# Linear attention on one core: later stores, part of relu(k) on GpSimd, eps added by 32-row matmuls, and a rewritten order of work

## The chip, the cores and the metric

The kernel runs on one core of one Trainium2 chip. The metric is the device time of one execution in microseconds. The kernel before took 180.35 us in the median of three runs (179.49, 180.35 and 180.47). The profiled execution, from which every duration in this text comes, took 179.64 us, and its span from the first to the last instruction is 177.9 us.

## The reference

Everything is bf16, with B=1, H=32 heads, S=2048 rows and D=128 columns.

```python
phi_q = jnp.where(q > 0, q + 1, jnp.exp(q)) + 1e-6
phi_k = jnp.where(k > 0, k + 1, jnp.exp(k)) + 1e-6
kv  = jnp.einsum("bhsd,bhse->bhde", phi_k, v)
z   = jnp.einsum("bhsd->bhd", phi_k)
num = jnp.einsum("bhqd,bhde->bhqe", phi_q, kv)
den = jnp.einsum("bhqd,bhd->bhq", phi_q, z)[..., None] + 1e-6
return num / den
```

Each of q, k, v and the output holds 16.8 MB, 512 KB per head, so that a head moves 2 MB and the whole kernel 67.1 MB.

## The kernel before

A head is split into 16 tiles of 128 rows. The feature map is written as phi(x) = min(exp(x), 1) + eps + relu(x), and the two summands are never added: TensorE multiplies by both of them and adds the products up in PSUM. One head h goes through these steps; each has a name that is used from here on.

- `ldk`, `ldq`, `ldv` (line 238): loads on SP's queue into rings of NI=8 heads. The load of head h+8 waits until head h has been read (`ek`, `rk`, `T`, `v1`).
- `ek` (line 347): ScalarE, exp(k) into `em_sb`. `em` (line 331): VectorE, min and eps in place, two heads in one instruction from head 4 on. `rk` (line 339): VectorE, relu(k) into `rk_sb`, also in pairs.
- `v1` (line 378): GpSimd copies v beside a column of ones, as 32-bit words. From head 3 on it waits for the reciprocal `rA` of three heads earlier.
- `kx`, `kv` (line 362): 32 matmuls build kv and z (129 columns) in one PSUM region. `kvs` (line 373): ScalarE copies it to SBUF.
- `T` (line 354): 16 transposes of q into the one PSUM buffer `xT`. `eq` (line 394): ScalarE, exp. `rqa` (line 399): ScalarE, relu of the first half of the columns; `rqb` (line 402): VectorE, relu of the second half. In every fourth head (an "A" in `RELU_Q = "SSSA"`) ScalarE does both halves in one wide `rqa` and there is no `rqb`. `emq` (line 406): VectorE, min and eps.
- `nB`, `nA`, `nC`: the numerators with the denominator as column 129. In each of six PSUM banks a small matmul of a matrix of ones by `epsr` (line 277, 128 rows, 2 or 3 columns) sets the denominators to eps, and then 2 matmuls per tile (lines 281 and 283) add the products, 32 in a head.
- `rA`, `rC` (line 303): reciprocals. `fA`, `fC` (line 307): VectorE multiplies the numerators in PSUM by them, 12 and 4 tiles, into `o_sb`, a ring of NO=6 heads. `st` (line 251) stores a head from there, and `fA` and `fC` wait for the store of six heads earlier.

The last two heads are cut into three parts each (D, B, C), and ScalarE scales the C part (line 324).

No loop runs on the chip. The order of each engine's queue is a list written out by hand in `SCHEDULE` (`PE`, `DVE`, `ACT`, `POOL`); a further list `kv` is the order in which the engines use the PSUM banks that kv and the last four tiles share. `Program.resolve` turns dependences across engines into semaphore waits. SP's queue is in the order of the program: after the first 8 heads, each turn gives three loads of head h+8 and, with `LAG = 2`, the store of head h-2:

```python
for h in range(NH + LAG - 1):
    if h + NI < NH:
        loads(h + NI)
    if h >= LAG:
        store(h - LAG)
```

Matmuls on a unit matrix (`warm0` with 48, `warm1` with 22; line 437) run before the first transposes and between them and the second ones.

Of the kernel before, what the change touches and what calls it, by code (L numbers as in the profile page):

```python
# [15 lines left out]
class Program:  # L16
# [20 lines left out]
    def resolve(self):  # L37
# [5 lines left out]
        for bank, keys in self.banks.items():  # L43
            order = self.schedule[bank]
            assert sorted(order) == sorted(keys), (bank, set(order) ^ set(keys))
            for a, b in zip(order, order[1:]):
                if self.ops[a]["eng"] != self.ops[b]["eng"]:
                    self.ops[b]["deps"].append(a)
        value, count = {}, {}
# [48 lines left out]
def _eps_pieces():  # L98

    import struct  # L100

    def bf(x):
        u = struct.unpack("<I", struct.pack("<f", x))[0]
        u = (u + 0x7FFF + ((u >> 16) & 1)) & 0xFFFF0000
        return struct.unpack("<f", struct.pack("<I", u))[0]

    a = bf(EPS / 128)
    b = bf(EPS - 126 * a)
    return a, b, bf(EPS - 126 * a - b)


def bass_standalone__linear_attn_elu__prompt_kernel(nc: bass.Bass, q: bass.AP, k: bass.AP, v: bass.AP, out: bass.AP):
# [8 lines left out]
    NO = 6  # L121
    L = NH - 1

    LAG = 2
    VLAG = 3
    VAFTER = "rA"
    VFROM = 3
    VTO = 31
    LATE = {L - 1: dict(D="DVE", B="DVE", C="ACT"), L: dict(D="DVE", B="DVE", C="ACT")}
    V1_DVE = 1  # L130
    FUSED = [0] * NH
# [4 lines left out]
    WARM1 = 22  # L136
    FIRST = [("k", 0), ("q", 0), ("v", 0)]
    RELU_Q = "SSSA" * (NH // 4)
# [3 lines left out]
            "warm0 T0 warm1 T1 kx0 kv0 nC0 nA0 T2 nB0 kx1 kv1 nC1 kx2 kv2 nA1 T3 nC2 nB1 kx3 kv3 nB2 nA2 T4 nC3 kx4 kv4 nB3 "  # L142
            "nA3 T5 nC4 kx5 kv5 nB4 nA4 T6 nC5 kx6 kv6 nB5 nA5 T7 nC6 kx7 kv7 nB6 nA6 T8 nC7 kx8 kv8 nB7 nA7 T9 nC8 kx9 kv9 "
            "nB8 nA8 T10 nC9 kx10 kv10 nB9 nA9 T11 nC10 kx11 kv11 nB10 nA10 T12 nC11 kx12 kv12 nB11 nA11 T13 nC12 kx13 kv13 "
            "nB12 nA12 T14 nC13 kx14 kv14 nB13 nA13 T15 nC14 kx15 kv15 nB14 nA14 T16 nC15 kx16 kv16 nB15 nA15 T17 nC16 kx17 "
            "kv17 nB16 nA16 T18 nC17 kx18 kv18 nB17 nA17 T19 nC18 kx19 kv19 nB18 nA18 T20 nC19 kx20 kv20 nB19 nA19 T21 nC20 "
            "kx21 kv21 nB20 nA20 T22 nC21 kx22 kv22 nB21 nA21 T23 nC22 kx23 kv23 nB22 nA22 T24 nC23 kx24 kv24 nB23 nA23 T25 "
            "nC24 kx25 kv25 nB24 nA24 T26 nC25 kx26 kv26 nB25 nA25 T27 nC26 kx27 kv27 nB26 nA26 T28 nC27 kx28 kv28 nB27 nA27 "
            "T29 kx29 kv29 nB28 nA28 T30 nC28 kx30 kv30 nA29 nB29 nC29 T31 kx31 kv31 nD30 nC30 nB30 nD31 nC31 nB31 ").split(),
        DVE=(  # L150
            "eps0 ones v1ones0 v1ones1 eps1 eps2 rk0 em0 emq0 rqb0 rk1 v10 emq1 rqb1 rk2 rC0 fC0 em1 em2 rk3 rqb2 emq2 rA0 "
            "fA0 em3 rC1 fC1 rk5 rC2 fC2 em5 rA1 fA1 emq3 rA2 fA2 rk7 rC3 fC3 rqb4 emq4 rA3 fA3 em7 rC4 emq5 rqb5 fC4 rA4 fA4 "
            "rk9 rC5 rqb6 emq6 fC5 rA5 fA5 em9 rC6 fC6 emq7 rA6 fA6 rk11 rC7 rqb8 emq8 fC7 rA7 fA7 em11 rC8 rqb9 emq9 fC8 rA8 "
            "fA8 rk13 rC9 rqb10 emq10 fC9 rA9 fA9 em13 rC10 emq11 fC10 rA10 fA10 rk15 rC11 rqb12 emq12 fC11 rA11 fA11 em15 "
            "rC12 rqb13 emq13 fC12 rA12 fA12 rqb14 rC13 emq14 fC13 rk17 rA13 fA13 emq15 rC14 fC14 em17 rA14 fA14 rk19 rC15 "
            "rqb16 emq16 fC15 rA15 fA15 em19 rC16 rqb17 emq17 fC16 rA16 fA16 rqb18 rC17 emq18 fC17 rk21 rA17 fA17 emq19 rC18 "
            "fC18 em21 rA18 fA18 rk23 rC19 rqb20 emq20 fC19 rA19 fA19 em23 rC20 rqb21 emq21 fC20 rA20 fA20 rqb22 rC21 emq22 "
            "fC21 rk25 rA21 fA21 emq23 rC22 em25 fC22 rA22 fA22 rk27 rC23 rqb24 emq24 fC23 rA23 fA23 em27 rC24 rqb25 emq25 "
            "fC24 rA24 fA24 emq26 rC25 rqb26 rk29 fC25 rA25 fA25 emq27 rC26 em29 fC26 rA26 fA26 rk31 rC27 rqb28 emq28 rA27 "
            "fA27 em31 rqb29 fC27 rA28 fA28 emq29 rC28 fC28 rqb30 emq30 rC29 fC29 rA29 fA29 emq31.0 emq31.1 rD30 fD30 rC30 "  # L160
            "rB30 fB30 rD31 fD31 rC31 rB31 fB31 ").split(),
        ACT=(
            "ek0.0 ek0 eq0 rqa0 ek1 eq1 kvs0 rqa1 ek2 eq2 kvs1 rqa2 ek3 kvs2 ek4 ek5 eq3 rqa3 kvs3 ek6 eq4 rqa4 kvs4 ek7 eq5 "
            "rqa5 kvs5 ek8 eq6 rqa6 kvs6 ek9 eq7 rqa7 kvs7 ek10 eq8 rqa8 kvs8 ek11 eq9 rqa9 kvs9 ek12 eq10 rqa10 kvs10 ek13 "
            "eq11 rqa11 kvs11 ek14 eq12 rqa12 kvs12 ek15 eq13 rqa13 kvs13 ek16 eq14 rqa14 kvs14 ek17 eq15 rqa15 kvs15 ek18 "
            "eq16 rqa16 kvs16 ek19 eq17 rqa17 kvs17 ek20 eq18 rqa18 kvs18 ek21 eq19 rqa19 kvs19 ek22 eq20 rqa20 kvs20 ek23 "
            "eq21 rqa21 kvs21 ek24 eq22 rqa22 kvs22 ek25 eq23 rqa23 kvs23 ek26 eq24 rqa24 kvs24 ek27 eq25 rqa25 kvs25 ek28 "
            "eq26 rqa26 kvs26 ek29 eq27 rqa27 kvs27 ek30 eq28 rqa28 kvs28 ek31 eq29 rqa29 kvs29 eq30 rqa30 kvs30 eq31.0 "
            "eq31.1 rq31.0 rq31.1 kvs31 fC30.12 fC30.13 fC30.14 fC30 fC31.12 fC31.13 fC31.14 fC31 stC31 ").split(),
        POOL=(  # L170
            "ident0 ident v11 v12 v13 v14 v15 v16 v17 v18 v19 v110 v111 v112 v113 v114 v115 v116 v117 v118 v119 v120 v121 "
            "v122 v123 v124 v125 v126 v127 v128 v129 v130 v131 ").split(),
        kv=(
            "kx0 kv0 kvs0 nC0 rC0 fC0 kx1 kv1 kvs1 nC1 kx2 kv2 kvs2 rC1 fC1 nC2 rC2 fC2 kx3 kv3 kvs3 nC3 kx4 kv4 rC3 fC3 kvs4 "
            "nC4 kx5 kv5 rC4 kvs5 fC4 nC5 kx6 kv6 rC5 kvs6 fC5 nC6 kx7 kv7 rC6 fC6 kvs7 nC7 kx8 kv8 rC7 kvs8 fC7 nC8 kx9 kv9 "
            "rC8 kvs9 fC8 nC9 kx10 kv10 rC9 kvs10 fC9 nC10 kx11 kv11 rC10 kvs11 fC10 nC11 kx12 kv12 rC11 kvs12 fC11 nC12 kx13 "
            "kv13 rC12 kvs13 fC12 nC13 kx14 kv14 rC13 kvs14 fC13 nC14 kx15 kv15 rC14 fC14 kvs15 nC15 kx16 kv16 rC15 kvs16 "
            "fC15 nC16 kx17 kv17 rC16 kvs17 fC16 nC17 kx18 kv18 rC17 kvs18 fC17 nC18 kx19 kv19 rC18 fC18 kvs19 nC19 kx20 kv20 "
            "rC19 kvs20 fC19 nC20 kx21 kv21 rC20 kvs21 fC20 nC21 kx22 kv22 rC21 kvs22 fC21 nC22 kx23 kv23 rC22 kvs23 fC22 "
            "nC23 kx24 kv24 rC23 kvs24 fC23 nC24 kx25 kv25 rC24 kvs25 fC24 nC25 kx26 kv26 rC25 kvs26 fC25 nC26 kx27 kv27 rC26 "  # L180
            "kvs27 fC26 nC27 kx28 kv28 rC27 kvs28 kx29 kv29 kvs29 fC27 nC28 kx30 kv30 rC28 fC28 kvs30 nC29 rC29 fC29 kx31 "
            "kv31 nC30 kvs31 rC30 fC30.12 fC30.13 fC30.14 fC30 nC31 rC31 fC31.12 fC31.13 fC31.14 fC31 ").split())
# [4 lines left out]
    with ExitStack() as es:  # L187
# [38 lines left out]
        add("DVE", "eps0", lambda g: g.memset(epsr[:], ea))  # L226
        add("DVE", "eps1", lambda g: g.memset(epsr[0:1, :], eb), ["eps0"])
        add("DVE", "eps2", lambda g: g.memset(epsr[32:33, :], ec), ["eps0"])
        add("DVE", "ones", lambda g: g.memset(ones[:], 1.0))
        for s in range(2):  # L230
            add("DVE", f"v1ones{s}", lambda g, s=s: g.memset(v1_sb[:, s, :, D:NC + 1], 1.0))


        def load(name, dst, src, h, freed, parts=1):
            n = NT // parts
            for r in range(parts):
# [3 lines left out]
                    [f.format(h - NI) for f in freed if h >= NI] + (GATE if f"{name}{h}" == "k1" else []), dma=f"{name}{h % NI}" if parts == 1 else f"{name}{h}.{r}")  # L240

        def loads(h):
            load("k", k_sb, kf, h, ["ek{}", "rk{}"])
            load("q", q_sb, qf, h, ["T{}"])
            load("v", v_sb, vf, h, ["v1{}"])

        def ld(name, h):
            return [f"ld{name}{h}.0", f"ld{name}{h}.1"] if h == 0 and name == "k" else [f"ld{name}{h}"]
# [5 lines left out]
        for name, h in FIRST:  # L254
            load(name, dict(k=k_sb, q=q_sb, v=v_sb)[name], dict(k=kf, q=qf, v=vf)[name], h, [], 2 if h == 0 and name == "k" else 1)
        for h in range(max(h for _, h in FIRST) + 1, min(NI, NH)):
            loads(h)
        for h in range(NH + LAG - 1):
            if h + NI < NH:
                loads(h + NI)  # L260
            if h >= LAG:
                store(h - LAG)
# [12 lines left out]
        def numerator(e, h, tiles):  # L275
            s = h % 2
            e.matmul(_ap(o_ps[:, :], SLOT[tiles[0]] + D, [[NC, len(tiles)]]), lhsT=ones[:], rhs=epsr[:, 0:len(tiles)],  # L277
                     start=True, stop=False, skip_group_check=True)
            for t in tiles:
# [10 lines left out]
        def num(which, h, banks, deps, bank=None):  # L290
            def f(e):
                for b in banks:
                    ins = numerator(e, h, BANKS[b])
                return ins
# [203 lines left out]
```

## Time and profile before

| | |
|---|---|
| median of three runs | 180.35 us |
| profiled execution | 179.64 us |
| its span | 177.9 us |
| busy: PE, weight loads, DVE, ACT, POOL | 163.9, 157.7, 155.8, 161.2, 33.1 us |
| DMA | 67.52 MB, mean 380 GB/s |
| ACT: exp of k, exp of q, relu of q, kvs | 61.7, 58.8, 38.5, 9.6 us |
| DVE: division, emq, rk, em, rqb, reciprocals | 77.2, 21.1, 19.8, 19.8, 16.1, 13.1 us |
| POOL: the copy of v | 32.4 us, 1046 ns each |

PE is TensorE, DVE VectorE, ACT ScalarE, POOL GpSimd, SP SyncE. Busy times are shares of an engine's own time, and a PE that is shown busy is not always at its peak, because matmuls overlap and their ends are modelled. Neighbouring instructions of an engine overlap a little at their ends, so that the distance between two starts says what one costs, and the printed duration is some 0.1 us more. The granted clock of TensorE is 1.00 in all stretches but the first twenty microseconds and the end.

### The profile page before, as it was taken

The numbers are of one execution on the slowest core, as the hardware profiler recorded it, in microseconds if no ns is written. First come the engines' busy times: TensorE is split into PE (matmuls) and PEld (weight loads), VectorE is DVE, ScalarE is ACT, GpSimd is POOL, SyncE is SP. The second block draws the span as 40 slices with busy tenths as digits, with TensorE's granted clock in tenths as the row PEclk, the third lists the DMA queues.
The fourth block names the chain that finished last, engine by engine and source line by source line (L and its number), as shares of the span: only waits on it lengthen the run. The fifth ranks groups of instructions, "written<-read, shape, count | busy, mean of one in ns | idle before, by whom it ended". The sixth has DMA issues, their size and how long they took to land.

```text
span 177.9 us, 6326 instructions
## 1 busy us (share of the span) xinstructions
PE 163.9 (92%) x2822; PEld 157.7 (89%) x2822; DVE 155.8 (88%) x230; ACT 161.2 (91%) x140; POOL 33.1 (19%) x37
## 2 busy tenths in 40 slices
PE   6849987999999999999999999999999899999981
PEld 6848886999999999999998999989999799999971
DVE  1255699799999999999999999999999899999983
ACT  5396999989999999999999999999999989996572
POOL 1022022222121222222121122222222022222000
PEclk9996999999999999999999999999999999999998
DMA  5999999999999999999999999999999999984336
GB/s 156 366 417 412 410 407 411 406 410 404 414 415 416 416 413 416 418 412 421 414 411 420 415 418 416 415 419 415 415 416 415 420 413 420 411 333 179 125 122 236
DMA packets 18891, 67.52 MB, mean 380 GB/s; under 512 B 2096, under 2 KB 2480, under 8 KB 18864
## 3 DMA queue, kind: packets, MB, share of 16 engines
q1 hardware_dynamic: 18720, 66.99, 93.7%
q8 instruction: 22, 0.36, 0.8%
q10 hardware_dynamic: 144, 0.13, 0.2%
q14 instruction: 5, 0.04, 0.1%
HBM read 50.33 MB, written 16.78 MB: 377 GB/s over the span
## 4 chain that ended last, share of the span: by engine, by line
ACT 48%; PE 20%; DVE 16%; DMA 12%; issue 1%; SPq 0%; DVEq 0%
ACT la L347 19%; ACT la L394 18%; PE la L362 9%; DMA out_dram<-la 9%; ACT la L399 8%; DVE la L307 8%; PE la L281 4%; PE la L283 3%; PE la L354 3%; DMA la<-in_q_dram 3%; ACT la L373 2%; DVE la L339 2%; DVE la L402 2%; DVE la L406 2%; DVE la L303 1%
## 5 line engine op out<-in xcount | busy, mean ns | idle before, releaser
L307 DVE TENSOR_TENSOR la<-la 128x512 bf16<-128x512 f32 (+2 forms) x64 | 77.2, 1206 | 3.7 <-DMA out_dram<-la 1.2
L283 PE MATMUL la<-la 128*128 128x129 bf16 x512 | 68.0, 220 | 0.0
L281 PE MATMUL la<-la 128*128 128x129 bf16 x512 | 68.0, 219 | 0.0
L362 PE MATMUL la<-la 128*128 128x129 bf16 x1024 | 65.5, 222 | 0.6 <-DVE la L307 0.5
L394 ACT ACTIVATE la<-la 128x2048 bf16<-128x2048 bf16 x31 | 58.8, 1895 | 5.1 <-PE la L354 3.0
L347 ACT ACTIVATE la<-la 128x2048 bf16<-128x2048 bf16 (+1 forms) x33 | 61.7, 1877 | 1.4 <-DMA la<-in_k_dram 1.4
L362 PEld LDWEIGHTS la<-la 128*128 128x128 bf16 x1024 | 61.3, 99 | 1.2 <-DVE la L307 0.8
L378 POOL COPY la<-la 128x1024 int32<-128x1024 int32 x31 | 32.4, 1046 | 128.7 <-DVE la L303 115.1
L283 PEld LDWEIGHTS la<-la 128*128 128x128 bf16 x512 | 49.5, 97 | 0.0
L281 PEld LDWEIGHTS la<-la 128*128 128x128 bf16 x512 | 47.1, 97 | 0.0
L399 ACT ACTIVATE la<-la 128x1024 bf16<-128x1024 bf16 (+1 forms) x31 | 38.5, 1241 | 0.0
L277 PE MATMUL la<-la 128*128 128x3 bf16 (+1 forms) x192 | 32.5, 169 | 5.1 <-DVE la L307 3.0
L354 PE MATMUL la<-la 128*128 128x128 bf16 x512 | 33.9, 219 | 3.0 <-DVE la L402 2.1
L354 PEld LDWEIGHTS la<-la 128*128 128x128 bf16 x512 | 29.6, 98 | 4.4 <-DVE la L402 3.2
L277 PEld LDWEIGHTS la<-la 128*128 128x128 bf16 x192 | 18.7, 97 | 9.1 <-DVE la L307 7.1
L406 DVE TENSOR_SCALAR la<-la 128x2048 bf16<-128x2048 bf16 x31 | 21.1, 682 | 5.8 <-ACT la L394 5.8
L339 DVE TENSOR_SCALAR la<-la 128x4096 bf16<-128x4096 bf16 (+1 forms) x18 | 19.8, 1100 | 3.0 <-DMA la<-in_k_dram 3.0
L331 DVE TENSOR_SCALAR la<-la 128x4096 bf16<-128x4096 bf16 (+1 forms) x18 | 19.8, 1098 | 1.0 <-ACT la L347 0.9
L402 DVE TENSOR_SCALAR la<-la 128x1024 bf16<-128x1024 bf16 x24 | 16.1, 673 | 2.1 <-ACT la L394 2.1
L303 DVE RECIPROCAL la<-la 128x4 f32<-128x4 f32 (+2 forms) x66 | 13.1, 200 | 2.9 <-PE la L283 2.6
L373 ACT ACTIVATE la<-la 128x129 bf16<-128x129 f32 x32 | 9.6, 301 | 3.1 <-PE la L362 1.6
L437 PE MATMUL la<-la 128*128 128x120 bf16 x70 | 6.2, 273 | 1.5 <-POOL la L222 1.5
(18 smaller groups left out, 16.1 us busy)
## 6 DMA issues: line engine op xcount, KB each, us to landing
la<-in_q_dram SPq DMA_DIRECT2D x32, 512.0 KB, 15.4
la<-in_v_dram SPq DMA_DIRECT2D x32, 512.0 KB, 15.8
la<-in_k_dram SPq DMA_DIRECT2D x31, 512.0 KB, 15.3
out_dram<-la SPq DMA_DIRECT2D x31, 512.0 KB, 15.2
la<-in_k_dram SPq DMA_DIRECT2D x2, 256.0 KB, 2.9
out_dram<-la SPq DMA_DIRECT2D x2, 192.0 KB, 2.1
out_dram<-la ACTq DMA_DIRECT2D x1, 128.0 KB, 1.9
```

What stands on the lines that cost most here:

```text
L277: e.matmul(_ap(o_ps[:, :], SLOT[tiles[0]] + D, [[NC, len(tiles)]]), lhsT=ones[:], rhs=epsr[:, 0:len(tiles)], start=True, stop=False, skip_ ...
L281: e.matmul(o, lhsT=emq_sb[:, s, t * P:(t + 1) * P], rhs=kvs_sb[:, s, :], start=False, stop=False, skip_group_check=True)
L283: ins = e.matmul(o, lhsT=rq_sb[:, s, t * P:(t + 1) * P], rhs=kvs_sb[:, s, :], start=False, stop=True, skip_group_check=True)
L307: add("DVE", f"f{which}{h}", lambda e: e.tensor_tensor(out=_ap(o_sb[:, :, :, :], ob + t0 * D, [[n * D, nb], [D, n], [1, D]]), in0=_ap(o_ps ...
L339: add("DVE", key, lambda e: e.tensor_scalar(rk_sb[:, s:s + n], k_sb[:, b:b + n], 0.0, None, op0=ALU.max), [d for i in range(n) for d in ld ...
L347: add("ACT", "ek0.0" if h == 0 and r == 0 else f"ek{h}", lambda e, c=c: e.activation(em_sb[:, h % 4, c], k_sb[:, h % NI, c], ACT.Exp), ([f ...
L354: ins = e.transpose(xT[:, j * P:(j + 1) * P], q_sb[:, h % NI, j * D:(j + 1) * D], ident[:])
L362: ins = e.matmul(kv_ps, lhsT=src[:, h % 4, j * D:(j + 1) * D], rhs=v1_sb[:, h % 2, j, 0:NC], start=(j + part == 0), stop=(j == NT - 1 and ...
L378: add("DVE" if h < V1_DVE else "POOL", f"v1{h}", lambda e, h=h, s=s: e.tensor_copy(v1_sb[:, s, :, 0:D].bitcast(i32), v_sb[:, h % NI].rearr ...
L394: add("ACT", f"eq{h}", lambda e, s=s: e.activation(emq_sb[:, s], xT[:, :], ACT.Exp), [f"T{h}"] + nums(h - 2))
L399: add("ACT", key, lambda e, s=s, c=c: e.activation(rq_sb[:, s, c], xT[:, c], ACT.Relu), [f"T{h}"] + nums(h - 2))
L406: add("DVE", f"emq{h}", lambda e, s=s: e.tensor_scalar(emq_sb[:, s], emq_sb[:, s], 1.0, EPS, op0=ALU.min, op1=ALU.add), [f"eq{h}"])
```

## The change

1. **Stores and output ring.** `NO` goes from 6 to 12 heads. `LAG` is now a list, 2 + h//3: after the loads of head h+8 the queue holds the stores up to head h-LAG[h], so the stores fall behind by one more head in every three. Ahead of the loads of the last head 14 stores stand in the queue (21 before), and the other 17 whole-head stores follow them.
2. **relu(k).** From head 4 on GpSimd does relu(k) of tiles 4 to 15 of each head (`rkp`, 128x1536, 28 instructions), and VectorE's `rk` of a pair is left with tiles 0 to 3 of two heads (2x512 columns). `kx` and `kv` also wait for `rkp`, and so do the loads of k eight heads on. A new list `after` makes every `v1` and `rkp` on GpSimd wait for a named VectorE instruction (`rk`, `em` or `emq`); the old wait for `rA` is gone.
3. **relu(q).** `RELU_Q` is "S" in all heads: the eight wide `rqa` (seven in heads 3 to 27, and the two halves of the last head) become half `rqa` plus a VectorE `rqb`, and in the last head VectorE alone does it.
4. **eps.** The ones-by-eps matmul of a bank uses 32 rows instead of 128, at row offset 32 times (bank mod 4), and the small matmuls of the two banks of a part come first, before all its products. The constants are written by 12 small memsets instead of 3.
5. **The start.** The first head's q comes in two loads, and `T`, `eq`, `emq`, `ek`, `em` and `rk` of head 0 in two halves each; `warm1` has 40 matmuls instead of 22, and a new `warm2` of 8 waits for `emq0` and stands before `T1`.
6. **The order.** All the lists of `SCHEDULE` are new.

```diff
+        for k, d in self.schedule.get("after", {}).items():
+            self.ops[k]["deps"].append(d)
...
-    NO = 6
+    NO = 12
-    LAG = 2
+    LAG = [2+h//3 for h in range(40)]
-    WARM1 = 22
+    WARM1 = 40
+    WARM2 = 8
+    HALF = "kq"
+    RKP = [()]*4+[((4,16),)]*(NH-4)
-    RELU_Q = "SSSA" * (NH // 4)
+    RELU_Q = "S" * 32
...
     PE=(
+            "warm0 T0.0 T0 warm1 warm2 T1 kx0 kv0 kx1 kv1 nC0 nB0 nA0 T2 kx2 kv2 nC1 nB1 nA1 T3 kx3 kv3 nC2 nA2 nB2 T4 nC3 "
...
     DVE=(
+            "fC21 emq22 rA21 fA21 rk25 rk27 rC22 rqb23 fC22 emq23 rA22 fA22 em27 rqb24 rC23 fC23 emq24 rA23 fA23 rqb25 rC24 "
+            "emq25 fC24 rA24 fA24 em29 rC25 rqb26 fC25 emq26 rA25 fA25 rk29 rC26 rqb27 fC26 emq27 rA26 fA26 rk31 rqb28 rC27 "
...
     ACT=(
+            "ek0.0 ek0 eq0.0 eq0 rqa0 ek1 eq1 kvs0 ek2 rqa1 kvs1 ek3 eq2 rqa2 ek4 kvs2 eq3 rqa3 ek5 kvs3 eq4 ek6 kvs4 rqa4 "
...
     after=
+            "rkp24<emq21 v123<emq21 v124<em25 rkp25<emq22 v125<rk27 rkp26<emq23 v126<em27 rkp27<emq24 rkp28<emq25 v127<em29 "
+            "v128<emq26 rkp29<rk29 v129<emq27 rkp30<emq28 v130<em31 v131<emq29 rkp31<emq30 ").split()),
...
-        for h in range(NH + LAG - 1):
-            if h + NI < NH:
-                loads(h + NI)
-            if h >= LAG:
-                store(h - LAG)
+        done = 0
+        for h in range(NH - NI):
+            loads(h + NI)
+            while done <= h - LAG[h]:
+                store(done)
+                done += 1
+        for h in range(done, L):
+            store(h)
...
+        def numerator(e, h, banks):
             s = h % 2
-            e.matmul(_ap(o_ps[:, :], SLOT[tiles[0]] + D, [[NC, len(tiles)]]), lhsT=ones[:], rhs=epsr[:, 0:len(tiles)],
-                     start=True, stop=False, skip_group_check=True)
-            for t in tiles:
+            for b in banks:
+                r, n = slice(32 * (b % 4), 32 * (b % 4) + 32), len(BANKS[b])
+                e.matmul(_ap(o_ps[:, :], SLOT[BANKS[b][0]] + D, [[NC, n]]), lhsT=ones[r, :], rhs=epsr[r, 0:n],
+                         start=True, stop=False, skip_group_check=True)
+            for t in [t for b in banks for t in BANKS[b]]:
...
+            c = slice(0, min([a for a, _ in RKP[h]] + [NT]) * D)
+            for i in range(n):
+                for r, (t0, t1) in enumerate(RKP[h]):
+                    add("POOL", f"rkp{h + i}" + (f".{r}" if r < len(RKP[h]) - 1 else ""), lambda e, i=i, t0=t0, t1=t1: e.tensor_scalar(
+                        rk_sb[:, s + i, t0 * D:t1 * D], k_sb[:, b + i, t0 * D:t1 * D], 0.0, None, op0=ALU.max),
+                        ld("k", h + i) + [prev("kv", h + i, 4), f">rkp{h + i}.{r - 1}" if r else None])
...
             add("DVE", key, lambda e: e.tensor_scalar(
-                rk_sb[:, s:s + n], k_sb[:, b:b + n], 0.0, None, op0=ALU.max),
+                rk_sb[:, s:s + n, c], k_sb[:, b:b + n, c], 0.0, None, op0=ALU.max),
```

## The prediction

> **What bounds the kernel now.** First the table of busy time by stretches, one row of the middle (start:end, length, then busy us and instructions of PE, weight loads, DVE, ACT and POOL, granted clock, DMA share, GB/s):
>
> ```profile
> 60.00:80.00 20.00, 19.84 (x355) 19.22 (x353) 19.48 (x28) 20.00 (x18) 4.16 (x4) 1.00 1.03 415
> ```
>
> In the middle ACT has no gap, DVE is at 97%, PE nearly always busy, and DMA moves 415 GB/s at a share of 1; only POOL is idle. So I price a head on every engine. ACT first, from the chain that ended last (start, us, work); it shows a wide ("A") head and a usual one:
>
> ```profile
> 66.42 1.79 ACT la L347
> 68.22 1.77 ACT la L394
> 69.98 1.77 ACT la L399
> 71.75 0.17 ACT la L373
> 71.92 1.80 ACT la L347
> 73.72 1.77 ACT la L394
> 75.48 0.91 ACT la L399
> 76.39 0.17 ACT la L373
> ```
>
> The chain lies on ACT from 37 to 125 us with few breaks. A usual head is 1.80+1.77+0.91+0.17 = 4.65, an "A" head 5.51, the mean of one in four 4.87. Then DVE's timeline, where the distance of starts is the cost:
>
> ```profile
> 97.56 1.76 DVE L307 TENSOR_TENSOR la<-la 128x1536 bf16<-128x1536 f32 x1
> 99.24 1.22 DVE L331 TENSOR_SCALAR la<-la 128x4096 bf16<-128x4096 bf16 x1
> 100.37 0.18 DVE L303 RECIPROCAL la<-la 128x4 f32<-128x4 f32 x1
> 100.46 0.66 DVE L402 TENSOR_SCALAR la<-la 128x1024 bf16<-128x1024 bf16 x1
> 101.04 0.68 DVE L406 TENSOR_SCALAR la<-la 128x2048 bf16<-128x2048 bf16 x1
> 101.64 0.69 DVE L307 TENSOR_TENSOR la<-la 128x512 bf16<-128x512 f32 x1
> 102.24 0.23 DVE L303 RECIPROCAL la<-la 128x12 f32<-128x12 f32 x1
> ```
>
> Per head: `fA` 1.68, `em` and `rk` 1.13 a pair, so 0.57 each, `rC` 0.09, `rqb` 0.58 in three heads of four, `emq` 0.60, `fC` 0.60, `rA` 0.26. Sum 4.81: DVE is as full as ACT. Last PE, where a product starts every 0.056 us and an eps matmul takes a slot of 0.03:
>
> ```profile
> 46.67 0.22 PE L283 MATMUL la<-la 128*128 128x129 bf16 x1
> 46.72 0.17 PE L277 MATMUL la<-la 128*128 128x3 bf16 x1
> 46.75 0.22 PE L281 MATMUL la<-la 128*128 128x129 bf16 x1
> ```
>
> With 32 kv matmuls in 1.84 (chain, at 148.34), 16 transposes in 0.89, 32 products in 1.79 and six eps in 0.16, PE needs 4.68 per head. DMA needs 2.1 MB / 415 GB/s = 5.05, more than all, but heads loaded ahead cover that.
>
> **relu(q) and the middle.** I measure the middle from ACT's `ek3` (22.39) to `ek31` (155.86): 133.5 us. Between them ACT does 28 `ek`, 26 `eq`, 26 `rqa` of which seven are wide, and 27 `kvs`: 50.4+46.0+29.7+4.6 = 130.7. The other 2.8 are idle or hand-offs, of which 1.2 are two waits of DVE on stores (below). The change halves seven wide `rqa`: 7 x 0.86 = 6.0 off, floor 124.7. It adds `rqb` to a quarter of the heads, 0.145 per head on DVE.
>
> **relu(k).** `rk` of a pair shrinks from 4096 to 1024 elements. Not in the trace, but the 2048 and 4096 forms cost 0.60 and 1.13, so on their line 0.33, 0.17 per head instead of 0.57; that it now lies in two pieces of 512 is in no row either, and at the 0.58 of `rqb`'s 1024 columns it would be 0.12 more per head, the spare of DVE. I take 0.33, since shape and engine are those of `rk`. DVE: 4.81+0.145-0.40 = 4.56, over 27 heads 123. The 128x1536 relu on POOL is in no row. POOL's 128x1024 copy takes 1.046: if the price is per element, 1.57; if per byte, 0.8; the affine select of 128 columns (0.29, against 0.10 for POOL's one-column memset) would give up to 2.4. I take 1.5, nearest to the big copy; with `v1`, POOL is at 2.6 of 4.7 per head, so its own time hides. `kx`, which now waits for it, has `kv` and then three numerators behind it on PE; but `rkp29`, started at `rk29`, has one `emq` and three numerators, about 4 us, before `kx29` is due, and most others have more. What does not hide is where it lies: in this trace every POOL copy after the start begins 0.03 us after an `fA`, and no row shows a SBUF-only instruction of DVE starting while POOL works. I bound that by "costs nothing" and by "the DVE instruction waits until POOL is done". For the second I added, for each named trigger in the list, the DVE work from it to the next `em`, `rk` or `emq` (mostly `rA fA` = 1.94, `rC rqb fC` = 1.27, or both) and compared it with the POOL work started there. At 1.5 us 12 of 44 places overrun, together 3.2 us (three instructions in 3.2, four in 4.9, `rkp29` in 1.27); at 1.9 8.8 us; at 2.4 19.5 us. DVE has 27 x 0.12 = 3.3 to spare under PE's 4.68, so I take nothing, and 3.2 as the upper end.
>
> [...]
>
> **eps.** Six slots of 0.03 per head; at best the second of each pair is free, 27 x 0.08 = 2.2 off PE. No row shows a 32-row matmul. At worst each change between row shapes lets PE wait for the matmul in flight: 0.22-0.056 = 0.164, six changes, 0.98 per head. The row nearest to it is the eps matmul itself, which goes between products of other width in 0.03; I take no change.
>
> [...]
>
> **The middle's sum.** Floors for 27 heads: PE 126.4, ACT 124.7, DVE 123 to 126. PE, off the path now, comes to bind. Before, 1.6 beyond the store waits was lost over the floor; I keep that: 128.0, so 5.5 off 133.5. Ends: 1.5 off (126.4 with three times the loss) and 8.3 off (ACT's floor with 0.5).
>
> **Stores.** What they cost now:
>
> ```profile
> 141.81 0.69 DVE L307 TENSOR_TENSOR la<-la 128x512 bf16<-128x512 f32 x1 [0.88 <-DMA out_dram<-la]
> ...
> 151.81 0.69 DVE L307 TENSOR_TENSOR la<-la 128x512 bf16<-128x512 f32 x1 [0.29 <-DMA out_dram<-la]
> ```
>
> A transfer lands 15 us after its issue because about 12 are in flight, and six buffers are just too few. That 1.2 is in the sum above. The rest of the edit is cover: `ldk31` has 93 loads and 21 stores before it, lands at 2+115 x 0.524/0.415 = 147, and a middle that is faster by 8 needs it at 148. With 14 stores it lands at 138. The price moves to the ring: `st14`, the last behind loads, lands at 2+111 x 0.524/0.415 = 142, and `fC26`, which needs it, comes after `eq27`, about 147. All 67.1 MB take 162 us, under the end. SP's new wait for `rkp` (head h, eight heads early) has nothing urgent behind it. Cost 0; if the cover is gone, each us late is a us.
>
> **The start.** ACT's two large gaps before the middle:
>
> ```profile
> 8.08 1.88 ACT L394 ACTIVATE la<-la 128x2048 bf16<-128x2048 bf16 x1 [2.67 <-PE la L354]
> ...
> 16.07 0.28 ACT L373 ACTIVATE la<-la 128x129 bf16<-128x129 f32 x1 [1.63 <-PE la L362]
> ```
>
> The first waits for the whole of q0 (landed at 6.97); half of it lets `T0.0` and `eq0.0` start, I estimate, 1.2 earlier. The second is `kv0`, which took 3.49 for 32 matmuls against 1.84 later, with the granted clock at 0.83 in that stretch after PE had idled 2.1 before `T1`. The 26 more warming matmuls fill that gap (26 x 0.056 = 1.5), so 1.6 goes. Sum 2.8; I take 2.5 since k2 and v1 land only at 11 to 12.5 and may be late next. Ends 1.0 and 3.5. The memsets end long before k0 lands at 3.4.
>
> **The end.** From `ek31` 22 us follow, on PE and then DVE (four parts of 0.88 and six reciprocals). The order stays; relu of q31 moves 2 x 0.58 to DVE and off ACT's 1.95. Taken as 0, ends -1 and +1.5.
>
> **Sum.** 177.9 - 5.5 - 2.5 = 169.9, with the 1.7 around the span 171.6; the profiled execution was 0.7 under the median shown.
>
> **Rivals.** (a) *Gain half eaten.* Four engines within 3% of one another lose more at hand-offs: middle 1.5 off, start 1.0 off, end +1: 176.4 + 1.7 = 178.1. For it: DVE's order is irregular, with up to four POOL instructions on one trigger. Against: today ACT and DVE are equally full and lose 1.6. (b) *Row shapes drain PE,* slower: 4.68+0.98 = 5.66 per head, 27 heads 153+1.6 against 133.5, minus the start's 2.5: 177.9+21.1-2.5+1.7 = 198. It decides from 4.98 per head, 0.05 per change. Against: the 0.03 slot. (c) *POOL's relu is long and locks DVE out,* slower: at 2.4 us DVE needs 123+19.5+1.6 = 144 against 133.5, 177.9+10.6-2.5+1.7 = 188; it decides from about 2.1 us. Then the edit would not run beside PSUM reads as meant. Against: the copy's 1.02 ns per element.
>
> **Numbers.** Forecast 0.66, (a) 0.19, (b) 0.06, (c) 0.06, and 0.03 for nothing measurable, within 0.5% (0.9 us), which is what a measurement of this kernel can tell. Faster is the first two, 0.85. All good ends together give 177.9-8.3-3.5-1+1.7 = 166.8; the range cuts that at 167.5 and reaches up to (a), 178.
>
> **What would show it.** Right: `rqa` all near 1.03, ACT under 155 busy; POOL's relu near 1.5 and DVE's `emq` unmoved at 0.68; no wait on stores; `kv0` in 1.9; kv to kv 4.7. Wrong: POOL over 2 us or DVE gaps ended by POOL; an eps slot over 0.1; ACT waiting for loads after 100 us.

## The result, and the profile after

The changed kernel takes **232.29 us** (median of four runs, 230.66 to 233.32) where the kernel before takes 180.41 beside it (179.49 to 181.05). The ratio is 1.2873, 95% interval 1.2767 to 1.2978: slower by 52 us. The forecast was 171.6 with a range up to 178.0, so it had the wrong sign. The profiled execution took 230.66 us with a span of 228.9, 51.0 longer than before.

In the lines of the changed kernel the steps have these numbers: `em` 364, `rk` 388, `emq` 454, `rqb` 449, `rkp` 381, `v1` 424, `fA` and `fC` 335, `rA` and `rC` 332, `kv` 411, `T` 401, `ek` 395, `eq` 441, `kvs` 418, the eps matmul 308, the products 312 and 314.

The busy time by stretches, the same row of the middle as before (start:end, length, then busy us and instructions of PE, weight loads, DVE, ACT and POOL, granted clock, DMA share, GB/s), and one from later:

```profile
60.00:80.00 20.00, 16.85 (x271) 15.07 (x270) 19.86 (x22) 15.02 (x14) 14.49 (x6) 1.00 1.02 408
140.00:160.00 20.00, 16.94 (x277) 15.38 (x274) 19.72 (x23) 13.04 (x11) 16.22 (x6) 1.00 0.81 278
```

DVE is busy for 19.86 of 20 us, as before, but does 22 instructions where it did 28. Its instructions got longer. ACT (15.02) and PE (16.85), full before at 20.00 and 19.84, now idle. The groups by line and form (after the bar: busy us, mean ns of one, then the idle time before them and who ended it) say which; first POOL's from the page, then DVE's:

```profile
L381 POOL TENSOR_SCALAR la<-la 128x1536 bf16<-128x1536 bf16 x28 | 115.0, 4111 | 21.5 <-DVE la L454 11.5
L424 POOL COPY la<-la 128x1024 int32<-128x1024 int32 x31 | 36.4, 1178 | 43.8 <-DVE la L360 14.6
```

```profile
L335 DVE TENSOR_TENSOR la<-la 128x1536 bf16<-128x1536 f32 x30 | 52.5, 1751 | 0.8
L454 DVE TENSOR_SCALAR la<-la 128x2048 bf16<-128x2048 bf16 x30 | 42.2, 1409 | 1.7 <-ACT la L441 1.7
L364 DVE TENSOR_SCALAR la<-la 128x4096 bf16<-128x4096 bf16 x14 | 38.9, 2782 | 0.0
L449 DVE TENSOR_SCALAR la<-la 128x1024 bf16<-128x1024 bf16 x31 | 20.6, 665 | 1.0 <-ACT la L441 1.0
...
L388 DVE TENSOR_SCALAR la<-la 128x1024 bf16<-128x1024 bf16 x14 | 17.8, 1274 | 0.0
```

`fA`, `emq` and `em` before:

```profile
L307 DVE TENSOR_TENSOR la<-la 128x1536 bf16<-128x1536 f32 x30 | 52.7, 1758 | 1.2
L406 DVE TENSOR_SCALAR la<-la 128x2048 bf16<-128x2048 bf16 x31 | 21.1, 682 | 5.8 <-ACT la L394 5.8
...
L331 DVE TENSOR_SCALAR la<-la 128x4096 bf16<-128x4096 bf16 x14 | 17.0, 1215 | 0.1
```

POOL's relu takes 4.11 us, not 1.5. Of DVE's work `fA` (1751 ns) and `rqb` (665), which read PSUM, are as before (1758 and 673). The three that read and write SBUF alone have grown: `emq` from 682 to 1409, `em` from 1215 to 2782, and `rk` to a mean of 1274 where half of its runs take 418 or less. That is 30 x 0.73 + 14 x 1.57 + 14 x 0.85 = 56 us more on DVE. The timeline shows how one of them grows:

```profile
42.06 4.07 POOL L381 TENSOR_SCALAR la<-la 128x1536 bf16<-128x1536 bf16 x1
42.84 0.68 DVE L335 TENSOR_TENSOR la<-la 128x512 bf16<-128x512 f32 x1
43.44 3.77 DVE L364 TENSOR_SCALAR la<-la 128x4096 bf16<-128x4096 bf16 x1
43.55 0.28 ACT L418 ACTIVATE la<-la 128x129 bf16<-128x129 f32 x1 [3.19 <-DVE la L335]
47.13 0.21 DVE L332 RECIPROCAL la<-la 128x12 f32<-128x12 f32 x1
...
155.10 4.08 POOL L381 TENSOR_SCALAR la<-la 128x1536 bf16<-128x1536 bf16 x1 [0.63 <-DVE la L454]
155.19 1.76 DVE L335 TENSOR_TENSOR la<-la 128x1536 bf16<-128x1536 f32 x1
156.86 2.60 DVE L388 TENSOR_SCALAR la<-la 128x1024 bf16<-128x1024 bf16 x1
```

Beside POOL's relu `fC` (0.68) and `fA` (1.76) take what they always take (means 0.686 and 1.751). `em`, begun at 43.44, ends 1.08 us after POOL's end (46.13): its own work, done after POOL. `rk`, begun at 156.86, ends 0.28 after POOL's end (159.18). So it goes for all 27 of DVE's instructions on SBUF alone that begin while a relu of POOL runs: each ends 1.08 (`em`), 0.55 (`emq`) or 0.28 us (`rk` and the last head's half `emq`) after the relu. The profile counts the waiting as DVE's busy time (3.77 for an `em` of 1.22), which is why DVE looks full.

PE's timeline answers to the one of before (from 46.67 us, in the prediction). The eps matmuls are now 32 rows high:

```profile
151.80 0.22 PE L312 MATMUL la<-la 128*128 128x129 bf16 x1
151.85 0.22 PE L314 MATMUL la<-la 128*128 128x129 bf16 x1
152.01 0.18 PE L308 MATMUL la<-la 32*128 32x3 bf16 x2
152.12 0.23 PE L312 MATMUL la<-la 128*128 128x129 bf16 x1
152.18 0.22 PE L314 MATMUL la<-la 128*128 128x129 bf16 x1
```

From the last product to the eps pair pass 0.16, from there to the next product 0.11, together 0.27 where a product's own slot is 0.056: 0.21 for two eps matmuls, which before took 0.05, so 0.16 more in each of the three parts of a head. Last the two gaps of ACT at the start:

```profile
6.91 2.17 ACT L441 ACTIVATE la<-la 128x1024 bf16<-128x1024 bf16 x2 [1.33 <-PE la L401]
...
14.19 0.28 ACT L418 ACTIVATE la<-la 128x129 bf16<-128x129 f32 x1
```

`eq0` begins at 6.91 (8.08 before) and `kvs0` at 14.19 without a wait (16.07).

### The profile page after: what moved, and what is told of

The parts are those of the page before. It is cut to its first block, busy times and chain, and to the rows that moved or that the text cites. A ratio compares the mean times of both kernels' runs of the same rounds, so it can differ in the third digit from the quotient of the medians.

```text
span 228.9 us, 6447 instructions
## 1 busy us (share of the span) xinstructions
PE 182.9 (80%) x2848; PEld 166.5 (73%) x2848; DVE 206.5 (90%) x251; ACT 157.5 (69%) x139; POOL 151.6 (66%) x65
## 4 chain that ended last, share of the span: by engine, by line
DVE 53%; PE 20%; issue 9%; POOL 8%; DMA 4%; ACT 3%; POOLq 2%; SPq 0%; DVEq 0%
DVE la L335 19%; DVE la L454 12%; DVE la L364 11%; PE la L411 10%; POOL la L381 6%; DVE la L449 5%; DVE la L388 4%; PE la L312 4%; DMA la<-in_q_dram 3%; PE la L314 3%; POOL la L424 3%; PE la L401 3%; ACT la L441 2%; DVE la L332 2%; POOLq L200 2%
## 5 line engine op out<-in xcount | busy, mean ns | idle before, releaser
L381 POOL TENSOR_SCALAR la<-la 128x1536 bf16<-128x1536 bf16 x28 | 115.0, 4111 | 21.5 <-DVE la L454 11.5
L411 PE MATMUL la<-la 128*128 128x129 bf16 x1024 | 68.3, 227 | 20.0 <-DVE la L332 6.0
L411 PEld LDWEIGHTS la<-la 128*128 128x128 bf16 x1024 | 63.7, 101 | 22.0 <-DVE la L332 7.3
L441 ACT ACTIVATE la<-la 128x2048 bf16<-128x2048 bf16 (+1 forms) x32 | 58.3, 1823 | 18.7 <-PE la L401 18.3
L312 PE MATMUL la<-la 128*128 128x129 bf16 x512 | 69.8, 223 | 0.0
L314 PE MATMUL la<-la 128*128 128x129 bf16 x512 | 68.8, 221 | 0.0
L395 ACT ACTIVATE la<-la 128x2048 bf16<-128x2048 bf16 (+1 forms) x33 | 61.4, 1859 | 5.8 <-PE la L411 4.0
L314 PEld LDWEIGHTS la<-la 128*128 128x128 bf16 x512 | 50.3, 98 | 0.0
L312 PEld LDWEIGHTS la<-la 128*128 128x128 bf16 x512 | 47.9, 98 | 1.5
L454 DVE TENSOR_SCALAR la<-la 128x2048 bf16<-128x2048 bf16 (+1 forms) x32 | 43.0, 1348 | 4.4 <-ACT la L441 4.4
L364 DVE TENSOR_SCALAR la<-la 128x4096 bf16<-128x4096 bf16 x14 | 38.9, 2782 | 0.0
L401 PEld LDWEIGHTS la<-la 128*128 128x128 bf16 x512 | 29.6, 98 | 9.6 <-DVE la L449 8.0
L446 ACT ACTIVATE la<-la 128x1024 bf16<-128x1024 bf16 x31 | 31.6, 1020 | 0.0
L308 PE MATMUL la<-la 32*128 32x3 bf16 (+1 forms) x192 | 17.0, 173 | 12.3 <-DVE la L335 6.1
L308 PEld LDWEIGHTS la<-la 32*128 32x128 bf16 x192 | 9.0, 91 | 23.6 <-DVE la L335 7.4
L449 DVE TENSOR_SCALAR la<-la 128x1024 bf16<-128x1024 bf16 x31 | 20.6, 665 | 1.0 <-ACT la L441 1.0
L388 DVE TENSOR_SCALAR la<-la 128x1024 bf16<-128x1024 bf16 x14 | 17.8, 1274 | 0.0
## 6 DMA issues: line engine op xcount, KB each, us to landing
out_dram<-la ACTq DMA_DIRECT2D x1, 128.0 KB, 2.0
```

Of the source, the lines that this page charges most:

```text
L312: e.matmul(o, lhsT=emq_sb[:, s, t * P:(t + 1) * P], rhs=kvs_sb[:, s, :], start=False, stop=False, skip_group_check=True)
L314: ins = e.matmul(o, lhsT=rq_sb[:, s, t * P:(t + 1) * P], rhs=kvs_sb[:, s, :], start=False, stop=True, skip_group_check=True)
L364: add("DVE", key, lambda e: e.tensor_scalar(em_sb[:, s:s + n], em_sb[:, s:s + n], 1.0, EPS, op0=ALU.min, op1=ALU.add), [f"ek{h + i}" for i ...
L381: add("POOL", f"rkp{h + i}" + (f".{r}" if r < len(RKP[h]) - 1 else ""), lambda e, i=i, t0=t0, t1=t1: e.tensor_scalar(rk_sb[:, s + i, t0 * ...
L395: add("ACT", key, lambda e, c=c: e.activation(em_sb[:, h % 4, c], k_sb[:, h % NI, c], ACT.Exp), l + o + [prev("kv", h, 4)])
L401: ins = e.transpose(xT[:, j * P:(j + 1) * P], q_sb[:, h % NI, j * D:(j + 1) * D], ident[:])
```

## The experiments

The theory from these lines has two parts. P: POOL's relu of 1536 columns takes 4.08 us, and DVE's instructions on SBUF alone wait until it ends; this makes the whole 52 us. E: the 32-row eps matmuls cost PE about half a microsecond per head, which is hidden under P. The rival is that the new order, or E alone, makes the loss. The first four kernels take each part out or put it in alone.

**relu(k) back on DVE.**

```diff
-    RKP = [()]*4+[((4,16),)]*(NH-4)
+    RKP = [()]*NH
...
+    SCHEDULE["POOL"] = [x for x in SCHEDULE["POOL"] if x[:3] != "rkp"]
...
```

> The changed kernel with all of relu(k) back on DVE; GpSimd keeps only the copies of v, everything else stays changed. Theory P (GpSimd's 4.08 us relu locks DVE's SBUF-only instructions out): these go back to their lengths (emq 0.68, em of a pair 1.22), and most of the 52 us go. What stays is theory E (32-row eps matmuls drain PE, about 0.23 us per part and 0.68 per head instead of 0.16): PE needs 5.20 per head against DVE's 4.96, so about 186 us, 183 to 190. Rival O (the new order of the queues is what is slow): stays above 215. Without E: about 180.

Measured 186.85, ratio 1.0388 (1.035 to 1.0427). DVE's groups by form:

```profile
L456 DVE TENSOR_SCALAR la<-la 128x2048 bf16<-128x2048 bf16 x30 | 20.4, 680 | 3.3 <-ACT la L443 3.2
L366 DVE TENSOR_SCALAR la<-la 128x4096 bf16<-128x4096 bf16 x14 | 17.3, 1236 | 0.0
L390 DVE TENSOR_SCALAR la<-la 128x4096 bf16<-128x4096 bf16 x14 | 16.9, 1216 | 0.0
```

`emq` and `em` are back at their lengths. The account closes: DVE loses the 56 of waiting and takes on 14 x (1.216 - 0.42) = 11 of relu, net 45; the span falls by 228.9 - 184.9 = 44.0. So P makes 45 of the 52 us and not the whole, and 7 us over the kernel before are left.

**eps by 128 rows**, two matmuls first as in the change:

```diff
-                e.matmul(..., lhsT=ones[r, :], rhs=epsr[r, 0:n],
+                e.matmul(..., lhsT=ones[:], rhs=epsr[:, 0:n],
```

> The changed kernel with eps by 128-row matmuls as before, their place (both of a part first) unchanged. Theory P with E as a second cost under cover: PE gets 0.5 us per head back, but DVE is what binds, so 225 to 232 us. Rival (E is the main cost): under 200 us.

Measured 233.7, ratio 1.2992 (1.2944 to 1.3041): a little above what was expected, and no gain (that it is 1.4 us more than the changed kernel's 232.29 is not explained). While DVE is held up, PE's half microsecond per head (3 x 0.16) is not on the path that sets the time.

**Both of these.**

> The changed kernel with both undone: relu(k) on DVE and eps by 128 rows. P and E together: DVE binds at 4.96 per head, 27 heads 134 and 1.6 lost against 133.5 before, the start 1.6 faster: about 180 us, 177 to 183. If order or stores cost something of their own: above 185.

Measured 179.8, ratio 1.0001 (0.9976 to 1.0026). Against the first kernel 128 rows now bring 7 us. PE's timeline:

```profile
79.88 0.22 PE L316 MATMUL la<-la 128*128 128x129 bf16 x1
79.94 0.19 PE L310 MATMUL la<-la 128*128 128x3 bf16 x2
79.99 0.22 PE L314 MATMUL la<-la 128*128 128x129 bf16 x1
```

The same order with eps of full height lets the next product start 0.11 after the last one, so that the two take 0.05, as before: it is the row shape, not the order of the two.

**The kernel before with the 32-row eps alone.**

```diff
-                ...lhsT=ones[:], rhs=epsr[:, 0:len(tiles)],
+                ...lhsT=ones[r, :], rhs=epsr[r, 0:n],      # r: 32 rows at 32 * (bank % 4); eps of both banks first
```

> The kernel before with the 32-row eps matmuls alone (the two of a part first, as in the change). Theory E: PE 5.20 per head, 27 heads 140 and 1.6 against 133.5, so about 188 us, 184 to 192, with 0.16 us between the last product of a part and the next eps matmul. Rival (only the order after relu(k) made PE look slow; row shapes are free): 179 to 181.

Measured 188.24, ratio 1.0465 (1.0424 to 1.0505). The row of its middle, and PE's timeline:

```profile
60.00:80.00 20.00, 20.00 (x334) 18.54 (x331) 18.66 (x26) 19.06 (x17) 4.16 (x4) 1.00 1.03 416
```

```profile
84.60 0.22 PE L287 MATMUL la<-la 128*128 128x129 bf16 x1
84.76 0.18 PE L281 MATMUL la<-la 32*128 32x3 bf16 x2
84.87 0.23 PE L285 MATMUL la<-la 128*128 128x129 bf16 x1
```

PE is at 20.00 of 20 with 334 matmuls where it did 355, so a head of 86 takes 5.15 us: PE binds. 27 x 5.15 = 139, and the middle (`ek3` to `ek31`) measures 139.7. Part E is shown. The trace also says where in the pair the cost lies: the second 32-row matmul, at another row offset, begins 0.003 us after the first (median of 92 pairs), where the second 128-row one in the run before begins 0.029 after. So the pair itself is cheap, and moving from one row offset to another within it costs nothing; the time goes between 128 rows and 32 (0.152 instead of 0.057 before the pair, 0.106 instead of 0.025 behind it).

**A relu on POOL that nobody needs.** To see P by itself, the kernel before gets, after each `v1`, a relu of k on POOL into a scratch tile that nothing reads, 1024 columns wide in one kernel and 512 in the other. The output is unchanged. The load of k eight heads on waits for the useless relu, and so does `kv` of three heads later; in neither trace does PE wait for POOL there. P says that DVE is held in every head; the rival, called L in the expectations, says that only late results cost.

```diff
+                add("POOL", f"dm{h}", lambda e, h=h: e.tensor_scalar(
+                    junk[:, h % 8], k_sb[:, h % NI, 0:8 * D], 0.0, None, op0=ALU.max), ld("k", h))
...
-            add("PE", f"kv{h}", ..., bank="kv")
+            add("PE", f"kv{h}", ... + ([f"dm{h - 3}"] if h >= 7 else []), bank="kv")
```

> The kernel before, all its work and order unchanged, with one useless GpSimd instruction per head from head 4 on: relu of 8 tiles of k (128x1024) into a scratch ring that nothing reads, right after the copy of v, which starts with fA. Theory P (GpSimd at 2.65 ns per column, and it locks DVE's SBUF-only instructions out while it runs): it ends 1.04+2.75 = 3.8 us after fA begins, the next em, rk or emq is due at 1.7, so 2.1 us per head, 28 heads: about 239 us, 225 to 245. Rival L (the change lost because the products waited for relu(k) or for GpSimd's late copies of v; there is no lock): POOL is at 3.8 of 4.9 per head and nobody needs the result, so 179 to 181.

> The same with 4 tiles (128x512), 1.4 us: it ends 2.45 us after fA begins, 0.75 past the window, 28 heads: P about 201 us, 194 to 206. Rival L: 179 to 181.

Measured 189.94 (ratio 1.0539, 1.0469 to 1.0609) for 1024 columns and 180.61 (1.0026, 0.9984 to 1.0069) for 512. Both expectations of the first miss; of the second's, P's misses and L's comes out. The timeline of the wider one, then that of the narrower:

```profile
95.40 2.77 POOL L384 TENSOR_SCALAR la<-la 128x1024 bf16<-128x1024 bf16 x1
96.05 0.94 DVE L411 TENSOR_SCALAR la<-la 128x2048 bf16<-128x2048 bf16 x1
...
97.79 1.46 DVE L333 TENSOR_SCALAR la<-la 128x4096 bf16<-128x4096 bf16 x1
...
100.44 3.01 POOL L384 TENSOR_SCALAR la<-la 128x1024 bf16<-128x1024 bf16 x1
101.09 1.47 DVE L341 TENSOR_SCALAR la<-la 128x4096 bf16<-128x4096 bf16 x1
```

```profile
99.12 2.32 POOL L384 TENSOR_SCALAR la<-la 128x512 bf16<-128x512 bf16 x1
99.76 1.22 DVE L333 TENSOR_SCALAR la<-la 128x4096 bf16<-128x4096 bf16 x1
```

With 1024 columns DVE came 0.65 us after POOL and lost only about 0.25 (`emq` at 96.05, `em` at 101.09); the instructions that came late in POOL's run waited to its end (`em` at 97.79 came 2.39 us after POOL and ends 1.08 after it). With 512 DVE, again 0.64 after POOL, lost nothing, and POOL was held instead: 2.32 where undisturbed ones take 1.49. So P as first put, "whoever comes second waits for the whole instruction", does not hold for short POOL instructions.

**4 tiles instead of 12 on POOL**, with eps by 128 rows:

```diff
-    RKP = [()]*4+[((4,16),)]*(NH-4)
+    RKP = [()]*4+[((12,16),)]*(NH-4)
```

> The changed kernel with eps by 128 rows and only 4 of 16 tiles of relu(k) on GpSimd (128x512, about 1.4 us), 12 on DVE. P: it fits most windows of DVE's work on PSUM (1.27 and 1.94 us); overruns sum to some 2.6 us, DVE saves 0.13 per head against relu(k) wholly on DVE: 178 to 180, within 1% of the kernel with both parts undone. If any GpSimd arithmetic hurts whatever its length: above 190.

Measured **177.77**, ratio 0.9857 (0.9807 to 0.9907): faster than both kernels, by 1.4% over the first, and just under the 178 to 180 that were expected. Its groups by form on DVE and on POOL:

```profile
L454 DVE TENSOR_SCALAR la<-la 128x2048 bf16<-128x2048 bf16 x30 | 21.4, 715 | 2.1 <-ACT la L441 1.8
...
L364 DVE TENSOR_SCALAR la<-la 128x4096 bf16<-128x4096 bf16 x14 | 17.2, 1225 | 0.0
L388 DVE TENSOR_SCALAR la<-la 128x3072 bf16<-128x3072 bf16 x14 | 13.4, 960 | 0.0
```

```profile
L381 POOL TENSOR_SCALAR la<-la 128x512 bf16<-128x512 bf16 x28 | 41.5, 1484 | 29.1 <-DVE la L454 15.6 <-DVE la L332 5.3 <-DVE la L388 5.2
```

The relu takes 1.48, and `emq` at 715 and `em` at 1225 ns are nearly at their own lengths: 30 x 0.035 + 14 x 0.010, about 1.2 us in all, against the 680 and 1215 of undisturbed ones.

**The kernel before with the new stores and 12 buffers alone** (the two edits of `NO` and `LAG` with their loop, as in the diff of the change).

> The kernel before with the stores' part alone (12 output buffers, stores that drop behind). The 1.2 us of DVE's waits on stores go: 0.5 to 1.5 us faster, ratio 0.992 to 0.998. Rival (transfers only shift): no change.

Measured 178.85, ratio 0.9932 (0.99 to 0.9965): a gain of 1.2 us, the size of the two store waits.

**Why 512, 1024 and 1536 columns behave differently.** Theory S: it is the size; a 1536-column relu holds DVE to its end even when DVE comes 0.64 us after its start. Theory W: it is when DVE comes; one that comes early gets through at any size, which with POOL at 1.04 + 4.08 = 5.1 us per head would make 190 to 210 us, and in the changed kernel DVE mostly came 1.2 to 3 us after POOL. The useless relu, now 1536 wide, tells them apart, since DVE comes at the same 0.64.

> The kernel before with the useless GpSimd relu now of 12 tiles (128x1536, 4.08 us), the changed kernel's own size. In the runs with 4 and 8 tiles DVE's next SBUF-only instruction came 0.64 us after the relu began and got in at once or 0.25 late; in the changed kernel it came 1.2 us or later and waited for GpSimd's end. Theory S (size: 1536 columns keep DVE out from the start to the end): about 3.4 us per head, above 250 us. [...]

Measured 265.13, ratio 1.474 (1.4676 to 1.4803). Its timeline:

```profile
94.33 4.08 POOL L384 TENSOR_SCALAR la<-la 128x1536 bf16<-128x1536 bf16 x1
94.97 4.51 DVE L333 TENSOR_SCALAR la<-la 128x4096 bf16<-128x4096 bf16 x1
99.40 0.16 DVE L305 RECIPROCAL la<-la 128x4 f32<-128x4 f32 x1
```

DVE came at 0.64 and waited for POOL's end at 98.41, 4.51 - 1.22 = 3.29 us. So did all 28 of DVE's instructions on SBUF alone that began during such a relu, from 0.63 to 2.94 us after its start. S stands: with the same order and the same moment, 1536 columns hold DVE and 512 do not. But the size is not all of it, for in the two narrower runs the moment decides. Beside 1024 columns the 30 that came up to 1.60 us after the relu's start got in, at most 0.3 late, and the 22 that came at 2.13 or later waited to its end. Beside 512 the 24 that came up to 0.71 got in at once, and the five that came from 0.93 on waited. Why, and why no such moment is found at 1536, these runs don't show.

**Two and three relus of 512 columns** in each head instead of one of 1024 or 1536, with eps by 128 rows:

```diff
-    RKP = [()]*4+[((4,16),)]*(NH-4)
+    RKP = [()]*4+[((8,12),(12,16))]*(NH-4)           # and ((4,8),(8,12),(12,16))
```

> The changed kernel with eps by 128 rows and 8 of 16 tiles of relu(k) on GpSimd, as two instructions of 128x512 instead of one long one. DVE has 4.68 per head, ACT 4.65, PE 4.68; GpSimd 1.04+2x1.49 = 4.0. If each short relu lets DVE in between: 174 to 180 us. If the pair acts as one hold of 3 us against windows of 1.3 and 1.9: 195 to 205 us.

> The changed kernel with eps by 128 rows and its 12 tiles of relu(k) on GpSimd, as three instructions of 128x512. GpSimd needs 1.04+3x1.49 = 5.5 per head, so it binds at 28 x (5.5-4.87) = 18 more than before at best. If the length of one instruction is what locks DVE out: 195 to 210 us. If GpSimd's total time does, however it is cut: 225 to 235 us.

Measured 188.4 (1.0482, 1.0442 to 1.0522) and 219.18 (1.2185, 1.2105 to 1.2265), each between its two expected ranges. With two, `emq` has 887 ns and `em` 1456: DVE is held less than by one long relu, but still held. With three POOL itself binds, in the row of its middle and in its waits (who waited for whom, us in total, times, longest):

```profile
60.00:80.00 20.00, 12.78 (x220) 12.16 (x218) 16.09 (x22) 13.58 (x11) 20.00 (x14) 0.94 1.03 416
```

```profile
PE la L413 <- POOL la L426: 22.8, 11, 7.2
```

So this placement does not work at 12 tiles in pieces either.

**What of POOL's price is the relu?** The kernel before with a useless POOL instruction on 512 columns, of four kinds in turn: copy, copy of the same bytes as 32-bit words, maximum as 16-bit integers, sum of two inputs.

```diff
+                add("POOL", f"dm{h}", (copy, copy as int32, max with 0 as int16, sum of two)[h % 4], ld("k", h))
```

> The kernel before with one useless GpSimd instruction per head on 128x512 columns of k as in the earlier run, its kind changing from head to head: copy of bf16, copy of the same bytes as int32 (256 words), max with 0 of the same bytes as int16, and a sum of two bf16 inputs. Only their shortest durations are wanted. If GpSimd's 2.6 ns per column is the price of arithmetic in this instruction: copy of bf16 about 0.5 us, int16 max like the bf16 relu, 1.49. If it is the price of a 2-byte element: copy of bf16 also 1.4 to 1.5, int32 0.3. Time near 180 us.

The single execution took 180.37, so none of the four costs time that one execution can show. In the trace an `em` that began 0.64 us after the sum of two still waited for its end (1.48 us where 1.22 is its own). POOL's groups by form:

```profile
L387 POOL TENSOR_SCALAR la<-la 128x512 int16<-128x512 int16 x7 | 16.3, 2322 | 0.0
L388 POOL TENSOR_TENSOR la<-la 128x512 bf16<-128x512 bf16 x7 | 7.3, 1040 | 0.0
L385 POOL COPY la<-la 128x512 bf16<-128x512 bf16 x7 | 4.3, 616 | 0.0
L386 POOL COPY la<-la 128x256 int32<-128x256 int32 x7 | 2.8, 403 | 0.0
```

The maximum has 2.32, which is again 1.49 and 0.83 of being held by `em`. So a copy of 512 columns takes 0.62, a sum of two tiles 1.04 and a maximum with a scalar 1.49. The copy, which stood as the row for the relu, is another price class; the type is not the reason, since the maximum as 16-bit integers has the 2.32 that the bf16 relu has when `em` holds it.

**Can the fastest version be balanced further?** The last two give ScalarE back the wide relu of q, in three heads of the 4-tile version (heads 7, 15, 23) and in seven heads of the version with neither cost (3, 7, ... 27), to relieve DVE.

```diff
-    RELU_Q = "S" * 32
+    RELU_Q = "".join("A" if h in (7, 15, 23) else "S" for h in range(32))
```

> The kernel with 4 tiles of relu(k) on GpSimd and eps by 128 rows (177.8 us), with ScalarE's wide relu(q) in heads 7, 15 and 23: DVE 4.82 to 4.76 per head, ACT 4.65 to 4.75, PE 4.68. If DVE binds: 1.0 to 1.6 us less, 176 to 177. If PE and the hand-offs bind: no change.

> The changed kernel with relu(k) wholly on DVE, eps by 128 rows and ScalarE's wide relu(q) in seven heads as before: start, stores and order are all that is left of the change. DVE 4.81, ACT 4.87 per head as before, the start 1.6 and the store waits 1.2 faster: 176.5 to 178.5. If the new order is no better than the old: 179 to 181.

Measured 178.44 (ratio 0.9919, 0.9892 to 0.9946) and 182.53 (1.0155, 1.0122 to 1.0187). The first gains nothing over the 4-tile version, the second is above both of its expected ranges and loses 2.7 to its own base of 179.8. So DVE's sum is not the only limit left. Why the wide relus hurt in the new order was not settled: from 60 to 80 us of the second PE, ACT and DVE are each at 18.0 to 19.3 of 20, and no one wait stands out.

## Why the prediction was wrong

The step that failed is the pricing of POOL's relu: 1.5 us and "nothing" for DVE, where the runs show 4.08 us and 56 us of DVE being held. Taken out alone it gives back 45 of the 52 us. The term for eps failed too, but its 7 us show only where the first cost is gone. By the prediction's own steps:

**The price of POOL's relu.** "I take 1.5, nearest to the big copy", ends 0.8 to 2.4; it is 4.08. This is the mis-sized term, by 2.6 us, with both ends far too low. The useless relus give 1.49, 2.76 and 4.08 for 512, 1024 and 1536 columns: about 0.2 + 2.5 ns per column. The copy of `v1` is 1.02 ns per column and of another operation. The row that pointed up, the affine select with its 0.29 for 128 columns, was taken as the far end; it still lay too low.

**Where it lies.** "I take nothing" for DVE being held. The method was right: at every place add up DVE's work on PSUM beside POOL's instruction and see what sticks out. Fed with 4.08 it gives 28 x (4.08 - 1.94), about 60 us, if every relu has the widest usual cover, and 66 added up place by place; measured 56. And in the 4-tile version, where the relu does take 1.48, DVE grows by about 1.2 us, inside the prediction's bounds of 0 and 3.2: given its price, this step would have held. Taken as a floor, DVE's 4.56 per head over 27 heads is 123, with 56 it is 179, and the middle of the changed kernel measures 178.7. So rival (c) came true, whose "decides from about 2.1 us" was on the right side; its price of 188 was that of 2.4 us. The bound "the DVE instruction waits until POOL is done" is what the 1536-column relu shows (3.29 us when DVE came 3.44 before its end); the 512- and 1024-column relus differ, since DVE, second by 0.65 us, lost 0 and 0.25 there and waited to the end only when it came later.

**eps.** "I take no change" for what stood between 2.2 off PE and 0.98 per head on it. Measured is 0.16 more per part, about 0.5 per head, so the cost that rival (b) names is there, at half its upper price; in the changed kernel it is hidden, since eps by 128 rows alone gained nothing (233.7). Its formula with that price gives 27 x (4.68 + 0.5) = 140 for the middle; the kernel with this edit alone has 139.7. Rival (b) put its threshold at 0.05 per change of shape; six changes at 0.08 are over it. The row taken as nearest, an eps matmul between products of another *width*, says nothing of another *height*. The prediction's best case came out in one half: the second matmul of a pair is nearly free (0.003), and the wait on both sides of the pair is what costs. The trace shows a wait at the change of rows (0.152 us before the pair instead of 0.057) and none from one offset to another (0.003); that PE drains in it, as rival (b) has it, no run here shows.

**The start.** 2.5 forecast. The same ACT work is done 1.6 us earlier in the changed kernel, 1.9 in the 4-tile version (`ek3` to `rqa2` end at 22.25, before at 24.20). `kv0` takes 2.00 instead of 3.49, near the forecast 1.9; the granted clock in its stretch is 1.00 (12 to 14.2 us) where it was 0.60 before (12 to 16 us; the 0.83 of the prediction is the mean from 10 to 20).

**The stores.** The waits on stores are gone, and the edit alone is worth the 1.2 that was put down for them. ACT's waits for loads after 100 us, named as a sign of trouble, are in none of the changed kernel, the version without both costs and the 4-tile version.

**relu(q) and the end.** `rqa` is 1.02 in all heads, as forecast. That the middle would fall to 128.0 with it is not borne out by any run; but no run has what it assumed, 12 tiles of relu(k) at 1.5 us on POOL, so how far it would then fall stays open. (Of its ends, "1.5 off" is added wrongly: 126.4 and three times 1.6 are 131.2, 2.3 off; it moves rival (a) and with it the upper end of the range by 0.8.) Where neither cost is there, it measures 133.6 with relu(k) on DVE and 131.6 with 4 tiles on POOL. DVE explains both sizes: 4.81 + 0.145 = 4.955 per head gives 133.8, and 0.135 less for `rk` at 3072 columns with 0.035 more for `emq` gives 131.1. It is an argument from sums, and the failed relief by ACT shows that DVE is not alone. The end, taken as 0, cost 1.5: from `ek31` the 4-tile version needs 26.3 us against 22.0, of which 2.85 are a head's `eq`, `rqa` and `kvs` that now come after it. Start -1.9, middle -1.9, end +1.5: -2.3, and the span fell by 2.2.

One of six parts of the change made 45 of the 52 us, and a second the 7 that are left when the first is out; each was one where no row of the profile showed the operation. Both were listed as rivals, at 6% each, because a single convenient row was taken for a bound.

## What to carry to other kernels

Here a row was a price only for its own operation and shape: the copy (0.62 us for 512 columns) did not price the maximum (1.49), and the matmul of another width (a slot of 0.03 us) did not price the one of another height (about 0.1). Where an edit moves work to an idle engine that may hold up the full one, price it by what sticks out of its cover, and ask at which duration it turns; here a relu of 1.5 us hid nearly whole and one of 4.1 us cost 2 us each time. And where DVE looks full, compare the mean length of each group with that of before: here DVE, held, showed as busy for 19.86 of 20 us, and `em` had gone from 1215 to 2782 ns.

## What was not expected of the hardware

- A maximum with a scalar on GpSimd takes 1.49 us for 512 columns, more than a sum of two tiles (1.04) and 2.4 times a copy (0.62).
- GpSimd and VectorE hold each other by size and by moment. 0.64 us after the start of a 512-column relu VectorE's `em` was not delayed and GpSimd lost 0.83; beside 1024 columns VectorE lost 0.25; beside 1536 it waited 3.29 us to the end. Beside 512 and 1024 columns those that came late (from 0.93 and 2.13 us on) waited to the end too. VectorE's reads of PSUM were not touched (`fA` 1751 ns against 1758).
- Three pairs of 32-row matmuls per head among 128-row ones cost 8 us of 180 (188.24 against 179.74); the same matmuls with 128 rows, in the same order, cost nothing that can be seen (0.05 us a pair, as before, and 179.8 in the version with neither cost). The second of such a pair, at another row offset, begins 0.003 us after the first.
